# Reordering preparation work around the QK projection, the folds, the router and the last row sums of a gated attention and PEER kernel

## The chip, the cores and the metric

The kernel runs on one core of one Trainium2 chip. The metric is device time in microseconds (us) of one execution, lower is better. A profile is one execution recorded by the hardware profiler; its span is the time from the first to the last instruction.

## What is computed

One token sequence x (2048 tokens of 1024) goes through two branches, mixed by a gate for each token. Branch a is self-attention with 32 heads of 32; branch b is a PEER layer: each token, for each of 32 heads, picks one of 64 experts by two small argmaxes over 8 keys, and adds the expert's row of v, weighted by a GELU of its dot product with the expert's row of u.

```python
g = sigmoid((x * gate_w).sum(-1, keepdims=True))
# branch a
q, k, v = split_heads(x @ wqkv)
o = softmax(q @ k.T * 32 ** -0.5) @ v
a = merge_heads(o) @ wo
# branch b, K = 1
q = einsum("nd,dhc->nhc", x, w_q)                 # two halves of 128
i1 = argmax(q[..., :128] @ k1.T); i2 = argmax(q[..., 128:] @ k2.T)
e = i1 * 8 + i2                                   # the softmax over one candidate is 1
act = gelu(einsum("nd,nhd->nh", x, u[e]))
b = einsum("nh,nhd->nd", act, v[e])
out = g * a + (1 - g) * b
```

## The kernel before

All matrix products of the projections are made in fp32r from two parts of each operand: a high part (ScalarE copies the fp32 value into the narrower type) and a low part (VectorE subtracts the high part from the value). A product takes three matmuls for each slice of the contraction: high by high, high by low, low by high. The helpers are `hi_of` (L134) and `lo_of` (L137) for parts, `x_hi`, `x_lo`, `w_hi`, `w_lo`, `w_parts` for those of one operand, and `split` (L93) for both at once.

The order of the instructions on each engine is the order in which the program writes them: the schedule is written by hand. Within an engine each instruction waits for those before it, and DMAs stand in the queue of the engine that issues them (SyncE by default, ScalarE or GpSimd where named).

**QK projection** (0 to about 382 us). The 2048 columns of the Q and K weights are eight chunks; the tokens are two passes of 1024. A unit is one chunk (a Q and a K block) by one pass. Units 0 and 8, the first of each pass, are computed plainly (`plain_mm`, `plain_group`) and leave through `plain_evac`; all others, `unit(u)` (L472), are one step of Strassen's scheme in Winograd's form: seven products P1 to P7 of half-size operands, of which some are sums (S1 to S4 of the weights, T1 to T4 of x). `product` (L286) makes one, twelve matmuls of 512 columns into a PSUM bank; six banks are used in turn. The order in a unit is P1, P5, P6, P2, P7, P3, P4. VectorE adds the products up, and `evac` (L248) writes a result as two parts to DRAM: the high part, then what is left over in the list `late` from the evacuation before (`run_late`, L239: a sum of squares on ScalarE that also reads the bank or writes over it, L246, and two DMAs on ScalarE's queue), then the low part. A bank is free for another product only when its squares are done. Between the products stand the turns: `ready(name)` prepares operands of the next unit, and `hook(name)` runs steps put down in `hooks` for one unit and product. The raw tiles are used again: T1 takes the place of B11, T3 of B12, T2 of B22, T4 of B21 in pass 0.

**Folds.** The PEER query weights are folded with the keys into 448 columns, since only differences of key scores are needed. `fold()` (L320) makes two of 32 parts by matmuls with `kpad`; after each fourth part ScalarE copies the bank to `wt` (L336) and the step goes on a list; `load_wqs` then loads the raw weights for the next two. `FOLDS` names the units with a fold at the end, `MID_FOLDS` those with one more after P2. `fold_t()` (L341), behind P5 of the next unit, transposes the copied bank on TensorE (L348), copies it out (L351) and writes it to the DRAM tensor `WPD` on GpSimd's queue. The 64 columns of u complete WPD; they are copied from DRAM to DRAM at L400.

**Router** (382 to about 470 us). `open_rw` (L646) loads WPD and `hi_wp`, `lo_wp` split it. For each tile of 128 tokens `router_mm` (L702) makes 24 matmuls, then `router_step(t)` (L754) runs a pipeline over tiles: `router_1` (ScalarE copies the u scores, VectorE finds maxima and marks them, GpSimd multiplies by ranks), `router_2` (VectorE), `router_3` (GpSimd), `router_4` (VectorE). Between the steps stand splits of the x tiles of other token quarters (`split_rx`, loaded by `load_rx`), and `bound` (L759) makes from the maxima of the squares (`sq`, `amax`, `pr`, `prm`) a limit for the scores. At t = 8 the program branches on it: `exact_maxima` (L775), with the branch at L786.

**Values and attention.** The V projection follows, then 32 heads of attention from 638 us to about 1670: scores to a ring of PSUM banks (L1286), exponentials on ScalarE (L1296), products with V (L1307), row sums by VectorE and DMA adds.

**Output projection.** The last head's row sums (`norm_sums`, L1354) go to DRAM (`smd`) and come back (`load_r`, `rr<-smd`), are turned into factors (`norm_r`) and come back again spread over the partitions (`rb`, `accd`). Until they are there the projection works on the other heads (`wo_mm`, L1486), with the PEER part from `load_at` (L1482) through `av_mm`; then it takes the last group (`split_o`, L1558).

Of the kernel before, what the change touches and what calls it, by code (L numbers as in the profile page):

```python
# [19 lines left out]
KC = D // 128  # L20
# [11 lines left out]
def gated_mha_peer_kernel(ctx, tc, xT, wqkv, wv, wo, wq, k12, ug, v, out):  # L32
# [367 lines left out]
    dma(WPD[:, :, 448:], ug.rearrange("p (k m) -> p k m", k=KC)[:, :, :64], nc.gpsimd)  # L400
# [3 lines left out]
    for kc in range(KC):  # L404
        if kc:
            split_x(kc)
        if kc in (1, 2):
            split_w0(2 * kc, 2 * kc + 2 if kc == 1 else KC)
        if kc + 4 < KC:
            load_x(0, kc + 4)  # L410
        if kc == 3:
            load_w(1)
        if kc == 4:
            for n in range(2):
                load_wq(n)
        if kc == HC:
            gate_mm(range(HC))
        if kc == KC - 2:
            gate_mm(range(HC, KC))
        if kc == KC - 1:  # L420
            x_sum(0, "T1")
            w_hi(1, "A11")
            x_hi(0, "T1")
            x_sum(0, "T3")
            w_lo(1, "A11")
            x_lo(0, "T1")
            w_sum(1, "S1")
            w_hi(1, "S1")
            w_sum(1, "S3")
            x_sum(0, "T2")  # L430
            w_lo(1, "S1")
            x_hi(0, "T2")
            w_sum(1, "S2")
            w_hi(1, "S2")
            w_lo(1, "S2")
            x_lo(0, "T2")
        order = [(n, i) for i in range(3) for n in range(2)]
        if kc in (0, KC - 1):
            order = [(n, i) for n in range(2) for i in range(3)]
        for w in range(2):  # L440
            for n, i in order:
                plain_mm(w, n, kc, i, kc == 0 and i == 0, kc == KC - 1 and i == 2)
# [5 lines left out]
    hooks = {}  # L448
    w_hi(1, "A12")
    w_lo(1, "A12")  # L450
    plain_evac(0, 1, 0)
    gate_out(0)
    x_sum(0, "T4")
# [5 lines left out]
    w_lo(1, "S3")  # L459
    w_hi(1, "S4")  # L460
    x_hi(0, "T4")
    w_lo(1, "S4")
    hooks[1, "P1"] = [(x_lo, 0, "T4"), (plain_evac, 0, 1, 1)]
    hooks[1, "P5"] = [(w_parts, 1, "A22"), (plain_evac, 0, 0, 0)]
# [3 lines left out]
    MID_FOLDS = {4, 10, 13}  # L468
# [3 lines left out]
    def unit(u):  # L472
# [69 lines left out]
        evac(1, c, n0, u2, p4)  # L542
        hook("P4")
        ready("P4")
        if u in FOLDS:
            fold(u != KC - 2)
# [80 lines left out]
    hooks[9, "P1"] = [(plain_evac, KC, 1, 1), (w_parts, nxt, "A22")]  # L627
# [16 lines left out]
    Wp, rwp = [], []  # L644

    def open_rw():  # L646
        wr.close()
        wqp.close()
        rw = Pool("rw", side="right")
        wpl, wph = ([rw.tile([128, HC, 512], F32R, name=f"wp{part}{i}") for i in range(2)] for part in "lh")  # L650
        for i in range(2):
            dma(wpl[i], WPD[:, i * HC:(i + 1) * HC, :])
            Wp.extend((wph[i][:, k, :], wpl[i][:, k, :]) for k in range(HC))
        rwp.extend((rw, wph, wpl))

    def hi_wp(i):
        hi_of((rwp[1][i],), rwp[2][i].bitcast(F32))

    def lo_wp(i):
        lo_of((rwp[1][i], rwp[2][i]), rwp[2][i].bitcast(F32))  # L660
# [9 lines left out]
    rw = rwp[0]  # L670
    assert not hooks and fold_no[0] == 32 and not pending


    blk = const.tile([128, 4], F32, name="blk")
    nc.vector.tensor_reduce(blk, ident.rearrange("p (j r) -> p j r", j=4), axis=AX.X, op=OP.max)
    pr = const.tile([128, KC], F32, name="pr")
    amax = const.tile([128, 2, KC], F32, name="amax")
    nc.vector.tensor_reduce(amax, sq, axis=AX.X, op=OP.max)
    nc.vector.tensor_mul(pr, amax[:, 0, :], amax[:, 1, :])
    nc.scalar.activation(pr, pr, AF.Sqrt)  # L680
    prm = const.tile([128, KC, 4], F32, name="prm")
    nc.vector.tensor_mul(prm, pr[:, :, None].to_broadcast([128, KC, 4]),
                         blk[:, None, :].to_broadcast([128, KC, 4]))
# [183 lines left out]
    rw.close()  # L867

# [870 lines left out]
```

## Time and profile before

| | us |
|---|---|
| three runs | 1853.41, 1857.26, 1858.73 |
| median | 1857.26 |
| profiled execution, its own time | 1857.74 |
| its span | 1856.0 |
| TensorE busy | 1826.5 |
| VectorE busy | 1457.1 |
| ScalarE busy | 1312.7 |
| GpSimd busy | 173.6 |
| mean granted TensorE clock | 0.994 |

A row of a timeline gives the start in us from the span's beginning, the length in us, the engine, the line of the program, the operation, output and inputs, how many were merged, and in brackets the engine's idle time just before and what ended it. A row of the list of waits gives who waited for whom, the total in us, how many times, and the longest. A row of a stretch gives for each engine the busy time and the number of instructions, then the granted TensorE clock (1.00 is full), the busy share of the 16 DMA engines and GB/s. PE is TensorE, DVE VectorE, ACT ScalarE, POOL GpSimd, SP SyncE. A row of a DMA queue gives packets, MB, and the share of all 16 engines' time in the stretch asked for.

### The profile page before, as it was taken

The numbers are of one execution on the slowest core, as the hardware profiler recorded it, in microseconds if no ns is written. First come the engines' busy times: TensorE is split into PE (matmuls) and PEld (weight loads), VectorE is DVE, ScalarE is ACT, GpSimd is POOL, SyncE is SP. The second block draws the span as 40 slices with busy tenths as digits, with TensorE's granted clock in tenths as the row PEclk, the third lists the DMA queues.
The fourth block names the chain that finished last, engine by engine and source line by source line (L and its number), as shares of the span: only waits on it lengthen the run. The fifth ranks groups of instructions, "written<-read, shape, count | busy, mean of one in ns | idle before, by whom it ended". The sixth has DMA issues, their size and how long they took to land.

```text
span 1856.0 us, 26459 instructions
## 1 busy us (share of the span) xinstructions
PE 1826.5 (98%) x10083; PEld 1106.0 (60%) x10083; DVE 1457.1 (79%) x1258; ACT 1312.7 (71%) x1716; POOL 173.6 (9%) x230
## 2 busy tenths in 40 slices
PE   9899999998999999999999999999999999999999
PEld 6677767787888744444444444444444444446887
DVE  7765875678877788888888888888888888884575
ACT  5544554441233499999999999999999999992221
POOL 1000000035301200000000000000000000000000
PEclk9999999999999999999999999999999999999999
DMA  7687697753247677767677777777777777775872
GB/s 266 201 282 257 233 290 248 229 177 104 80 140 253 240 174 159 177 155 180 156 183 174 161 183 165 184 172 180 166 178 169 163 161 180 185 135 165 278 174 82
DMA packets 135633, 345.24 MB, mean 186 GB/s; under 512 B 17168, under 2 KB 57904, under 8 KB 116112
## 3 DMA queue, kind: packets, MB, share of 16 engines
q1 hardware_dynamic: 95696, 193.41, 35.1%
q0 software_dynamic: 17984, 112.36, 27.9%
q10 hardware_dynamic: 21824, 37.76, 6.8%
q8 instruction: 80, 1.31, 0.3%
q14 instruction: 49, 0.40, 0.1%
HBM read 171.76 MB, written 72.36 MB: 132 GB/s over the span
## 4 chain that ended last, share of the span: by engine, by line
PE 63%; issue 7%; DMA 2%; DVE 2%; POOL 1%; ACT 1%; SPq 0%; DVEq 0%; POOLq 0%; ACTq 0%
PE ring L1286 27%; PE o L1307 25%; PE pa L932 6%; PE pa L1491 1%; PE ring L1320 1%; PE bk L709 1%; PE pa L1498 1%; DVE acc L1336 1%; DMA smd<-ssb 1%; DMA rb<-rd 1%; POOL eq L723 1%; DMA accd<-rd 0%; DMA t1l<-xl 0%; DVE xl L95 0%; DVE xh L938 0%
## 5 line engine op out<-in xcount | busy, mean ns | idle before, releaser
L1296 ACT ACTIVATE P<-ring 128x1024 f32<-128x1024 f32 (+2 forms) x1031 | 913.0, 985 | 14.6 <-DMA accd<-P 1.1
L1336 DVE TENSOR_TENSOR acc<-acc,P 128x2048 f32<-128x2048 f32 x319 | 730.9, 2291 | 73.2 <-ACT P L1296 48.0
L1307 PE MATMUL o<-P,V 128*32 128x512 f32 x3840 | 464.8, 599 | 0.0
L1286 PE MATMUL ring<-Q,K 98*128 98x512 f32 x1024 | 272.5, 407 | 0.5 <-ACT P L1296 0.5
L1286 PE MATMUL ring<-z,z 98*128 98x512 f32 x1020 | 270.5, 407 | 0.6 <-ACT accd L1296 0.6
L1286 PEld LDWEIGHTS ring<-Q,K 98*128 98x128 f32 x1024 | 181.9, 188 | 145.3 <-ACT P L1296 73.3
L1286 PEld LDWEIGHTS ring<-z,z 98*128 98x128 f32 x1020 | 181.4, 188 | 142.5 <-ACT P L1296 72.3
L1307 PEld LDWEIGHTS o<-P,V 128*32 128x32 f32 x3840 | 98.8, 109 | 223.3 <-issue 214.4
L1329 POOL DMA_DIRECT2D accd<-P x95 | 81.5, 857 | 931.7 <-ACT P L1296 414.0
L1334 DVE TENSOR_TENSOR acc<-P,P 128x2048 f32<-128x2048 f32 x32 | 73.4, 2292 | 74.5 <-ACT P L1296 74.5
L292 PE MATMUL bk<-xh,S 128*128 128x512 f32 x336 | 83.7, 401 | 2.8 <-ACT bk L246 2.8
L292 PE MATMUL bk<-xh,A 128*128 128x512 f32 x336 | 82.8, 395 | 0.0
L292 PE MATMUL bk<-xl,S 128*128 128x512 f32 x336 | 80.2, 390 | 2.2 <-ACT bk L246 2.2
L292 PEld LDWEIGHTS bk<-xh,A 128*128 128x128 f32 x336 | 62.1, 188 | 23.8 <-issue 7.5
L135 ACT ACTIVATE hi<-u 128x512 fp32r<-128x512 f32 x42 | 26.5, 632 | 69.5 <-DVE u L498 68.0
L292 PEld LDWEIGHTS bk<-xh,S 128*128 128x128 f32 x336 | 64.0, 193 | 17.4 <-ACT bk L246 3.3
L292 PEld LDWEIGHTS bk<-xl,S 128*128 128x128 f32 x336 | 62.9, 188 | 17.3 <-ACT bk L246 2.6
L1339 DVE TENSOR_TENSOR acc<-acc,accd 128x2048 f32<-128x2048 f32 x32 | 73.1, 2284 | 0.0
L1296 ACT ACTIVATE accd<-ring 128x1024 f32<-128x1024 f32 (+2 forms) x64 | 62.3, 1034 | 2.3 <-PE ring L1286 2.2
L932 PE MATMUL pa<-woh,acc 128*128 128x512 f32 x192 | 62.2, 389 | 0.0
L138 DVE TENSOR_TENSOR A<-wraw,A 128x512 fp32r<-128x512 f32 x42 | 28.9, 688 | 32.0 <-ACT A L135 32.0
L498 DVE TENSOR_TENSOR u<-u,bk 128x512 f32<-128x512 f32 x70 | 46.6, 682 | 5.3 <-PE bk L292 2.6
(300 smaller groups left out, 2138.9 us busy)
## 6 DMA issues: line engine op xcount, KB each, us to landing
accd<-P POOLq DMA_DIRECT2D x95, 1024.0 KB, 7.6
wqt<-in_wq SPq DMA_DIRECT2D x64, 512.0 KB
wraw<-in_wqkv SPq DMA_DIRECT2D x28, 512.0 KB
kdh<-hi ACTq DMA_DIRECT2D x32, 256.0 KB
kdl<-lo ACTq DMA_DIRECT2D x32, 256.0 KB
qdh<-hi ACTq DMA_DIRECT2D x32, 256.0 KB
qdl<-lo ACTq DMA_DIRECT2D x32, 256.0 KB
z<-kdh SPq DMA_DIRECT2D x32, 256.0 KB
```

Of the source, the lines that this page charges most:

```text
L135: nc.scalar.activation(parts[0], src, AF.Copy)
L138: nc.vector.tensor_tensor(out=parts[1], in0=src, in1=parts[0].bitcast(F32), op=OP.subtract)
L292: nc.tensor.matmul(ps, a[i][:, k, :], b[j][:, k, :], start=(k == 0 and i == j == 0), stop=(k == HC - 1 and i == 1))
L498: nc.vector.tensor_tensor(out=out, in0=a, in1=b, op=OP.add)
L932: nc.tensor.matmul(ps, self.a[a][i][:, k, :], self.b[b][j][k], start=(not first and k == 0 and i == j == 0), stop=(k == HC - 1 and i == 1))
L1286: on_ring(nc.tensor.matmul(ring[:, i, :], K[:98, kt * 128:(kt + 1) * 128], Q[:98, qc * 512:(qc + 1) * 512], start=True, stop=True), i)
L1296: on_ring(nc.scalar.activation(P[h, kt][:, q0 * 512:(q0 + m) * 512].rearrange("p (a m) -> p a m", a=m), ring[:, i:i + m, :], AF.Exp, scale ...
L1307: nc.tensor.matmul(O[h][32 * qc:32 * qc + 32, :], Vt[g][:, kt, 32 * j:32 * j + 32], p[:, qc * 512:(qc + 1) * 512], start=(kt == 0), stop=( ...
L1329: nc.gpsimd.dma_start(ACCD[h], P[h, kt], accum_op=OP.add)
L1334: nc.vector.tensor_add(ACC[h], P[h, 0], P[h, kt])
L1336: nc.vector.tensor_add(ACC[h], ACC[h], P[h, kt])
L1339: nc.vector.tensor_add(ACC[h], ACC[h], ACCD[h])
```

## The change

It adds and removes no matmul. In the order of the program:

- The copy of u's columns into `WPD` moves from the beginning of GpSimd's queue to behind unit 0's evacuations.
- The operand steps between units 0 and 1 are written in another order. They were ahead of the last group of plain matmuls in the text and are now behind it, which by itself changes no engine's order; the sum T4 comes before S2, the first steps of A12 before those of S2, `x_lo` of T4 out of unit 1; a `run_late` comes before S4's low part, and one behind A22's parts in units 1 and 9; A22 moves from P5's hook to P1's in unit 1.
- A unit's fold comes before P4's hook and turn, no longer after them; the middle fold of unit 10 moves to unit 11.
- `WPD` is loaded behind P6 of unit 14 into a pool in the place of the folds' loads (`load_wp`, pool `rwl`); its split and that of the x tile `n1` (`hi_n1`, `lo_n1`) are spread over unit 15, where `n1` was split behind the unit.
- The norms' small steps move from in front of the router to its steps 2 and 3 (`norms`, `spread_norms`); `router_step` runs `router_1` of the new tile before `router_2` of the one before.
- `load_at` for the first two token blocks comes behind `load_r` of the last row sums.

```diff
-    dma(WPD[:, :, 448:], ug.rearrange("p (k m) -> p k m", k=KC)[:, :, :64], nc.gpsimd)
...
-        if kc == KC - 1:
-            x_sum(0, "T1")
...
-            w_sum(1, "S3")
-            x_sum(0, "T2")
-            w_lo(1, "S1")
-            x_hi(0, "T2")
-            w_sum(1, "S2")
-            w_hi(1, "S2")
-            w_lo(1, "S2")
-            x_lo(0, "T2")
...
     hooks = {}
+    x_sum(0, "T1")
...
+    w_sum(1, "S3")
+    x_sum(0, "T2")
+    w_lo(1, "S1")
+    x_hi(0, "T2")
+    x_sum(0, "T4")
+    w_sum(1, "S2")
     w_hi(1, "A12")
+    w_hi(1, "S2")
+    x_lo(0, "T2")
+    w_lo(1, "S2")
     w_lo(1, "A12")
     plain_evac(0, 1, 0)
     gate_out(0)
-    x_sum(0, "T4")
     x_hi(0, "T3")
     x_lo(0, "T3")
     plain_evac(0, 0, 1)
     w_hi(1, "S3")
     w_sum(1, "S4")
     w_lo(1, "S3")
+    x_hi(0, "T4")
     w_hi(1, "S4")
-    x_hi(0, "T4")
+    run_late()
     w_lo(1, "S4")
-    hooks[1, "P1"] = [(x_lo, 0, "T4"), (plain_evac, 0, 1, 1)]
-    hooks[1, "P5"] = [(w_parts, 1, "A22"), (plain_evac, 0, 0, 0)]
+    x_lo(0, "T4")
+    hooks[1, "P1"] = [(plain_evac, 0, 1, 1), (w_parts, 1, "A22"), (run_late,)]
+    hooks[1, "P5"] = [(plain_evac, 0, 0, 0)]
+    dma(WPD[:, :, 448:], ug.rearrange("p (k m) -> p k m", k=KC)[:, :, :64], nc.gpsimd)
...
-    MID_FOLDS = {4, 10, 13}
+    MID_FOLDS = {4, 11, 13}
...
         evac(1, c, n0, u2, p4)
+        if u in FOLDS:
+            fold(u != KC - 2)
         hook("P4")
         ready("P4")
-        if u in FOLDS:
-            fold(u != KC - 2)
...
-    hooks[9, "P1"] = [(plain_evac, KC, 1, 1), (w_parts, nxt, "A22")]
+    hooks[9, "P1"] = [(plain_evac, KC, 1, 1), (w_parts, nxt, "A22"), (run_late,)]
...
-    def split_n1():
-        XS.update({(0, 0): X["B11"], (0, 1): X["B21"], (1, 1): X["B22"],
-                   (1, 0): x_parts("xh1", XR["n1"], xp)})
+    def hi_n1():
+        XS.update({(0, 0): X["B11"], (0, 1): X["B21"], (1, 1): X["B22"], (1, 0): x_parts("xh1", None, xp)})
+        hi_of(XS[1, 0], XR["n1"])
+
+    def lo_n1():
+        lo_of(XS[1, 0], XR["n1"])
+
+    def load_wp():
+        wqp.close()
+        pools.append(Pool("rwl", side="right"))
+        for i in range(2):
+            wl_.append(pools[0].tile([128, HC, 512], F32R, name=f"wpl{i}"))
+            dma(wl_[i], WPD[:, i * HC:(i + 1) * HC, :])
 
     def open_rw():
         wr.close()
-        wqp.close()
-        rw = Pool("rw", side="right")
-        wpl, wph = ([rw.tile([128, HC, 512], F32R, name=f"wp{part}{i}") for i in range(2)] for part in "lh")
-        for i in range(2):
-            dma(wpl[i], WPD[:, i * HC:(i + 1) * HC, :])
...
+        pools.append(Pool("rw", side="right"))
+        wh_.extend(pools[1].tile([128, HC, 512], F32R, name=f"wph{i}") for i in range(2))
...
-    hooks[14, "P1"] = [(load_n1,)]
-    hooks[15, "P1"] = [(open_rw,)]
-    hooks[15, "P2"] = [(hi_wp, 0), (lo_wp, 0)]
-    hooks[15, "P7"] = [(hi_wp, 1), (lo_wp, 1)]
+    hooks[14, "P6"] = [(load_n1,), (load_wp,)]
+    hooks[15, "P1"] = [(open_rw,), (hi_wp, 0)]
+    hooks[15, "P5"] = [(lo_wp, 0), (hi_wp, 1)]
+    hooks[15, "P6"] = [(lo_wp, 1), (hi_n1,)]
+    hooks[15, "P2"] = [(lo_n1,)]
...
     run_late()
-    split_n1()
...
     def router_step(t):
-        for lag, f in ((3, router_4), (2, router_3), (1, router_2), (0, router_1)):
+        for lag, f in ((3, router_4), (2, router_3), (0, router_1), (1, router_2)):
...
+    def norms():
+        nc.vector.tensor_reduce(blk, ident.rearrange("p (j r) -> p j r", j=4), axis=AX.X, op=OP.max)
+        nc.vector.tensor_reduce(amax, sq, axis=AX.X, op=OP.max)
+        nc.vector.tensor_mul(pr, amax[:, 0, :], amax[:, 1, :])
+        nc.scalar.activation(pr, pr, AF.Sqrt)
+
+    def spread_norms():
+        nc.vector.tensor_mul(prm, pr[:, :, None].to_broadcast([128, KC, 4]),
+                             blk[:, None, :].to_broadcast([128, KC, 4]))
...
         router_step(t)
+        if t == 2:
+            norms()
+        if t == 3:
+            spread_norms()
         if t == 4:
             bound()
...
     load_o(1, 0, KC - 1, nc.gpsimd)
-    for n in range(2):
-        load_at(n)
     split_hi(1)
     for kc in range(1, KC - 1):
         split_hi(kc + 1)
         if kc == 1:
             norm_sums(H - 1, sm)
             load_r(G - 1)
+            for n in range(2):
+                load_at(n)
             pso.close()
```

More of the change, by code (lines that the diff above doesn't have):

```diff
@@ L448, in gated_mha_peer_kernel @@
     hooks = {}
+    x_sum(0, "T1")
+    w_hi(1, "A11")
+    x_hi(0, "T1")
+    x_sum(0, "T3")
+    w_lo(1, "A11")
+    x_lo(0, "T1")
+    w_sum(1, "S1")
+    w_hi(1, "S1")
+    w_sum(1, "S3")
[4 more added lines that the diff above has]
+    w_sum(1, "S2")
     w_hi(1, "A12")
+    w_hi(1, "S2")
+    x_lo(0, "T2")
+    w_lo(1, "S2")
     w_lo(1, "A12")
@@ L638, in load_n1 @@
         XR["n1"] = load_quarter(1, 0, x8.tile([128, HC, 512], F32, name="x8"))
[L640 to L644 removed]
+    def hi_n1():
[3 more added lines that the diff above has]
+        lo_of(XS[1, 0], XR["n1"])
+    wl_, wh_, pools = [], [], []
+    def load_wp():
[4 more added lines that the diff above has]
+            dma(wl_[i], WPD[:, i * HC:(i + 1) * HC, :])
     def open_rw():
         wr.close()
[L648 to L654 removed]
+        pools.append(Pool("rw", side="right"))
+        wh_.extend(pools[1].tile([128, HC, 512], F32R, name=f"wph{i}") for i in range(2))
     def hi_wp(i):
[L657 removed]
+        hi_of((wh_[i],), wl_[i].bitcast(F32))
     def lo_wp(i):
[L660 to L665 removed]
+        lo_of((wh_[i], wl_[i]), wl_[i].bitcast(F32))
+    hooks[14, "P6"] = [(load_n1,), (load_wp,)]
[3 more added lines that the diff above has]
+    hooks[15, "P2"] = [(lo_n1,)]
     for u in range(KC + 1, NUNIT):
@@ L668, in gated_mha_peer_kernel @@
     run_late()
-    split_n1()
-    rw = rwp[0]
+    rwl, rw = pools
+    Wp = [(wh_[i][:, k, :], wl_[i][:, k, :]) for i in range(2) for k in range(HC)]
     assert not hooks and fold_no[0] == 32 and not pending
     blk = const.tile([128, 4], F32, name="blk")
-    nc.vector.tensor_reduce(blk, ident.rearrange("p (j r) -> p j r", j=4), axis=AX.X, op=OP.max)
     pr = const.tile([128, KC], F32, name="pr")
     amax = const.tile([128, 2, KC], F32, name="amax")
-    nc.vector.tensor_reduce(amax, sq, axis=AX.X, op=OP.max)
-    nc.vector.tensor_mul(pr, amax[:, 0, :], amax[:, 1, :])
-    nc.scalar.activation(pr, pr, AF.Sqrt)
     prm = const.tile([128, KC, 4], F32, name="prm")
-    nc.vector.tensor_mul(prm, pr[:, :, None].to_broadcast([128, KC, 4]),
-                         blk[:, None, :].to_broadcast([128, KC, 4]))
     prf = prm.rearrange("p c j -> p (c j)")
@@ L867, in gated_mha_peer_kernel @@
     rw.close()
+    rwl.close()
     zp = Pool("zp", side="right")
```

7 lines of the change are left out of this document (removed).

## The prediction

> **What bounds the kernel now.** I read the page's first part, then the list of who waited for whom on TensorE, then the timelines of TensorE, ScalarE, VectorE and SyncE around each wait, and the DMA queues.
>
> ```profile
> PE 1826.5 (98%) x10083; PEld 1106.0 (60%) x10083; DVE 1457.1 (79%) x1258; ACT 1312.7 (71%) x1716; POOL 173.6 (9%) x230
> ```
> ```profile
> PE bk L348 <- ACT x L336: 5.4, 3, 3.9
> PE bk L292 <- ACT bk L246: 5.0, 2, 2.8
> PE bk L709 <- DVEq L786: 4.8, 1, 4.8
> PE pa L1491 <- ACT z L94: 4.4, 1, 4.4
> PE bk L280 <- ACT xh L94: 1.5, 1, 1.5
> ...
> PE bk L331 <- DMA wqt<-in_wq: 0.6, 1, 0.6
> PE bk L709 <- DVE wpl L138: 0.5, 1, 0.5
> ```
>
> TensorE is busy for all but 29.5 us of the 1856.0 us span, so nearly everything else is hidden behind it, and a change that adds no matmul can gain only in these waits (columns: us in total, times, longest). The seven rows hold 22.2 us. The change touches the place of each of them: line 348 is the transpose in `fold_t`, which waits for ScalarE's copy of the fold (L336); line 292 is a QK product that waits until a bank's squares (L246) are done; L709 with L786 is the router at the branch of `exact_maxima`; L1491 is the output projection; L280 the very first products.
>
> A long wait costs more than itself:
>
> ```profile
> 52.52 3.01 PE L292 MATMUL bk<-xh,S 128*128 128x512 f32 x12 [2.83 <-ACT bk L246]
> ...
> 72.43 1.11 PE L348 MATMUL bk<-ident,x 128*128 128x128 f32 x4 [3.90 <-ACT x L336]
> 73.20 5.22 PE L292 MATMUL bk<-xh,S 128*128 128x512 f32 x12
> ```
> ```profile
> 70.00:80.00 10.00, 7.57 (x24) 6.20 (x25) 7.20 (x12) 6.21 (x14) 0.80 (x1) 0.66 0.96 301
> ```
>
> After 2.83 us of idle time twelve matmuls take 3.01 us; after 3.90 us the next twelve take 5.22, and the granted clock of that stretch is 0.66. So a wait of 3.90 carries a surcharge of 2.2 us, one of 2.83 none. I take 3.4 us, the middle, as the point from which the surcharge falls due.
>
> **A, the folded weights' load out of the first microseconds.**
>
> ```profile
> wpd<-in_ug POOLq DMA_DIRECT2D x1, 256.0 KB, 5.5
> ```
> ```profile
> q0 software_dynamic: 61, 0.12, 40.2%
> ```
> ```profile
> q0 software_dynamic: 83, 0.15, 25.6%
> ```
> ```profile
> 8.20 0.63 ACT L94 ACTIVATE xh<-xh 128x512 fp32r<-128x512 f32 x1 [2.34 <-DMA xh<-in_xT]
> ```
>
> The two queue rows are the stretches 4 to 6 and 6 to 8 us: GpSimd's queue, nearly all of it this one 256 KB copy, takes 0.80 + 0.51 = 1.3 us of all 16 engines just while ScalarE waits for the second half of the first x tile, and TensorE behind it for 1.5 us. Bounds of the gain: 0 (if the x load was not behind it) and 1.5; I take **1.1**, near the queue's own 1.3. In its new place the copy stands on GpSimd's queue behind the four gate writes, beside unit 1's products; what it delays there by 1.3 us (the next fold's weights) is used a whole unit of seven products later. Without that cover it costs 1.3.
>
> **B, the turns ahead of unit 1, and the fold ahead of P4's turn.**
>
> ```profile
> 43.48 1.92 ACT L135 ACTIVATE xh<-xh 128x2048 fp32r<-128x2048 f32 x1 [3.96 <-DVE x L152]
> ```
> ```profile
> 40.51 0.68 DVE L138 TENSOR_TENSOR lo<-bk,hi 128x512 fp32r<-128x512 f32 x1
> 41.11 2.28 DVE L152 TENSOR_TENSOR x<-x,xh 128x2048 f32<-128x2048 f32 x1
> ```
> ```profile
> 71.29 0.61 ACT L135 ACTIVATE S<-wraw 128x512 fp32r<-128x512 f32 x1
> 71.81 0.57 ACT L336 ACTIVATE x<-bk 128x512 f32<-128x512 f32 x1
> ```
>
> Before, T3's high part (43.48) waits 3.96 us for the sum T4 (41.11), which stands on VectorE behind T2's low part, three short weight steps, a wait for one of them and an evacuation (40.51). The change puts that sum in front of them. Counting VectorE's instructions again in the new order (a wide one holds it 2.2 to 2.3 us, a narrow one 0.60, from 40.51 to 41.11), the sum is done before 37.5 and T2's low part, whose raw tile T3's high part overwrites, at 40.2. So T3's high part starts at about 40.3, 3.2 us earlier, and everything in order behind it with it. The new `run_late` behind A22 takes back 0.5: its write of a low part stands in ScalarE's queue until VectorE has made that part, and the next evacuation's copy is queued behind. Left: 2.7. Two waits follow from this. The squares that held P7 (2.83 us) now run before P7 comes: that wait goes whole. Then `fold_t` in unit 2 is late next: its copy at 71.81 stood behind two weight copies at 0.52 each (71.29 is the second); it now stands ahead of them, so it ends 2.7 + 1.04 = 3.7 earlier, while TensorE arrives 2.8 earlier. The wait of 3.90 becomes 3.0, TensorE goes on 3.7 earlier, and if 3.0 stays below the 3.4 also without the slow dozen: 3.7 + 2.2 = **5.9**. Bounds 3.2 (no more than the chain's shift) and 6.9.
>
> **C, units 9 to 13.** The second wait on squares (5.0 - 2.8 = 2.2) stands in unit 9; the added `run_late` lets those squares run before the next evacuation, so it goes. But again `fold_t` comes next:
>
> ```profile
> 255.22 0.57 ACT L336 ACTIVATE x<-bk 128x512 f32<-128x512 f32 x1
> ```
>
> Its copy moves ahead of two weight copies here too, 1.04 us, and no more, since VectorE's chain there doesn't move: of the 2.2 only **1.0** is kept. The third such wait (unit 13, the longer of the 1.5 that the two others share, 1.1) has one copy less in front: **0.5**. The fold moved from unit 10 to unit 11 leaves unit 10's wait for weights (0.6), yet unit 11 gets the same close pair of folds: between 0 and 0.6, I take **0.3**.
>
> **D, unit 15 and the router.**
>
> ```profile
> 394.68 16.11 SPq L76 DMA_DIRECT2D rx<-in_xT  x4
> ```
> ```profile
> 399.61 1.92 ACT L94 ACTIVATE xh<-rx 128x2048 fp32r<-128x2048 f32 x1 [3.96 <-DMA rx<-in_xT]
> ```
> ```profile
> 427.35 0.22 ACT L713 ACTIVATE xu<-bk 128x64 f32<-128x64 f32 x1 [5.22 <-PE bk L709]
> 432.79 0.22 ACT L713 ACTIVATE xu<-bk 128x64 f32<-128x64 f32 x1 [5.22 <-PE bk L709]
> ```
> ```profile
> 392.36 2.29 DVE L95 TENSOR_TENSOR xh<-x,xh 128x2048 fp32r<-128x2048 f32 x1 [2.49 <-ACT xh L94]
> ...
> 413.14 0.61 DVE L717 TENSOR_REDUCE m<-bk 128x64 f32<-128x448 f32 x1
> ...
> 419.69 0.61 DVE L717 TENSOR_REDUCE m<-bk 128x64 f32<-128x448 f32 x1
> ...
> 437.03 0.22 DVE L722 TENSOR_SCALAR eq<-m 128x64 f32<-128x64 f32 x1
> ```
>
> TensorE makes a router tile each 5.44 us (427.35 to 432.79). VectorE is finished with tile 7 at 437.25, 8 us after it could be, and the branch holds TensorE from 432.8 until then. The lag is there from the start: tile 0 is ready 8 x 5.44 us before 432.79, at 389.3, while VectorE is busy with n1's split until 394.65 and then with the norms. The change does that split inside unit 15, where VectorE has no weights to prepare, and starts the weight split a product earlier; VectorE is then free at about 386, before tile 0. SyncE's rx loads, which start at 394.68, the moment that split frees its raw tile, go out some 9 us earlier and land before 395, when step 1 asks for them. From there: a step that holds a split takes 6.55 us (413.14 to 419.69), 4.26 without its 2.29, of which I count 0.5 as waiting for GpSimd that the new order takes out. Seven steps to tile 7 are 7 x 3.8 + 4 x 2.2 (splits) + 0.9 (norms) + 1.0 (bound) = 37.3 us, in 38.1 available; the square root, now in front of a split on ScalarE, adds about 2. So VectorE passes the branch at 430.5 to 431.5 and TensorE arrives at 432.3. I leave 0.3 us for the branch (437.25 to 437.52 now). Gain: 4.8 - 0.3, the 0.5 of the wpl wait, and the surcharge 2.2 of a wait longer than 3.9: **7.2**. Bounds 0.5 and 7.5.
>
> **E, the last row sums.**
>
> ```profile
> 1674.10 3.74 SPq L76 DMA_DIRECT2D at<-atd  x2
> 1677.93 1.15 SPq L76 DMA_DIRECT2D smd<-ssb  x1
> 1689.13 0.31 SPq L76 DMA_DIRECT2D rr<-smd  x1
> ```
> ```profile
> DMA packets 27, 0.05 MB, mean 25 GB/s; under 512 B 1, under 2 KB 4, under 8 KB 27
> ```
> ```profile
> DMA packets 17, 0.02 MB, mean 8 GB/s; under 512 B 3, under 2 KB 16, under 8 KB 17
> ```
>
> The two loads stand on SyncE's queue in front of the write of the last sums (smd), on which the 4.4 us wait hangs. They hold it up by some 2.4 us at issue. But the write lands only at 1689.1, and the packet rows of 1686 to 1688 and 1688 to 1690 show why: a trickle of 2 KB packets (an earlier write) until 1688, then 1 KB packets (the two loads) for about 0.7 us, then the sums. Issued earlier, they still stand behind the 2 KB packets. Gain **0.7** (bounds 0.5 and 2.4); the wait becomes 3.7, above 3.4, and keeps its surcharge. The loads, now behind the wait for smd, come late by at most what the same wait covers.
>
> **The sum** is 1.1 + 5.9 + 1.8 + 7.2 + 0.7 = 16.7 us. The profiled execution took 1857.74 us (span 1856.0), 0.5 above the median of the three runs, 1857.26; nothing in the attention stage is touched, so it moves as a whole: 1857.74 - 16.7 = 1841.0, or 1840.5 by the median.
>
> **The rivals.** *The clock falls after the 3.0 us wait too.* For it: 3.0 is near 3.4. Then 2.2 less: 1842.7. Chance 0.18.
>
> *The clock looks at fixed stretches of time.* If what counts is an idle stretch of fixed length on a grid that doesn't know the kernel, then a wait of 3.7 us mostly straddles two, and E's surcharge goes as well: 1838.3. Against it: 3.90, 4.4 and 4.8 are only a little longer, and 3.90 was enough. Chance 0.13. The Trainium skill, "TensorE: Matmul & The Clock Gate", Part 1, says that: a free-running window of about 3.4 us, and half rate after an idle one; its sum would be the 1838.3, and the trace agrees with it at 2.83 and speaks half against it at 3.90, which would seldom hold a whole window.
>
> *VectorE still comes late to the branch*, because the rx loads are held by another tile of the closed pools and land near 399.6 as now. Then the square root's stall is added to the old lag and D gives no more than the 0.5: 1840.5 + 6.7 = 1847.2. Chance 0.12.
>
> *Slower: VectorE becomes the router's bound.* The new order makes each step wait for its tile first; if GpSimd's product beside VectorE's two-input instructions stretches every step to the 6.55 us of one with a split, the 15 tiles behind the first take 15 x 1.11 = 16.7 us more, and D's 7.2 is lost: 1840.5 + 23.9 = 1864.4. It decides from a mean step over 5.44. Against it: my count is 37.3 in 38.1. Chance 0.05.
>
> *The change moves waits and no more*: other in-order work turns up in each place, and the time stays within 3 us of before. Chance 0.05.
>
> **How the numbers follow.** My forecast has 0.47 and gives 1840.5 us. 0.3% is 5.6 us, about what a measurement of this kernel can tell from no change. Faster by more than that: 0.47 + 0.18 + 0.13 + 0.12 = 0.90; within: 0.05; slower: 0.05. The range takes in the three nearest rivals with the bounds of A and E: 1836.5 to 1849.5.
>
> **What would show it.** In the list of waits: L246 gone; L348 at about 3.0 + 1.5 + 0.6; DVEq L786 under 1 us; L1491 about 3.7; L280 under 0.6. The dozen after `fold_t` in unit 2 near 3.0 us, the router's first reduction near 388 before all shifts. Wrong: a wait on L786 of over 2 us, a copy L336 later than 69 us, a new wait on S3 or A22 in the units behind a fold, or an attention stage that isn't as long as before.

## The result and the profile after

The changed kernel takes 1848.07 us (median of 12 runs, 1844.77 to 1852.13) where the kernel before took 1857.08 beside it: a ratio of 0.9956, 95% interval 0.9946 to 0.9965. It is 9.0 us faster by the medians and 8.2 by the ratio (6.5 to 10.0). 16.7 were forecast. The profiled execution has a span of 1847.2 us against 1856.0.

The list of who waited for whom on TensorE, after (total us, times, longest):

```profile
PE bk L348 <- ACT x L336: 7.9, 3, 4.0
PE pa L1506 <- ACT z L94: 3.4, 1, 3.4
PE bk L771 <- DVE prm L766: 2.8, 1, 2.8
...
PE bk L280 <- ACT xh L94: 1.2, 2, 0.7
PE pa L947 <- ACT z L94: 1.2, 1, 1.2
...
PE bk L292 <- ACT bk L246: 0.3, 1, 0.3
```

The waits on squares (L246) and at the branch (L786 before) are gone but for 0.3 us each, as forecast. But the waits on the fold's copy (L348) grew from 5.4 to 7.9, and two rows are new: L771, the bound's matmuls, and a second wait on z at L947. The first products (L280) still wait 1.2 where under 0.6 was forecast.

TensorE's timeline, after, at P7 of unit 1, at the fold's transposes in units 2, 10 and 13, in the router, at the branch and in the output projection:

```profile
49.07 2.88 PE L292 MATMUL bk<-xh,S 128*128 128x512 f32 x12
...
69.00 1.11 PE L348 MATMUL bk<-ident,x 128*128 128x128 f32 x4 [4.03 <-ACT x L336]
69.76 5.39 PE L292 MATMUL bk<-xh,S 128*128 128x512 f32 x12
...
253.01 0.66 PE L348 MATMUL bk<-ident,x 128*128 128x128 f32 x4 [2.39 <-ACT x L336]
...
321.31 0.66 PE L348 MATMUL bk<-ident,x 128*128 128x128 f32 x4 [1.51 <-ACT x L336]
...
408.83 0.22 PE L771 MATMUL bk<-ones,prm 128*32 128x1 f32 x2 [2.85 <-DVE prm L766]
...
409.78 1.05 PE L709 MATMUL bk<-wph,xh 128*128 128x512 f32 x2
...
433.00 0.47 PE L709 MATMUL bk<-wph,xh 128*128 128x512 f32 x1 [0.30 <-ACT xu L713]
...
1688.12 1.19 PE L1506 MATMUL pa<-woh,z 128*128 128x512 f32 x4 [3.35 <-ACT z L94]
...
1725.71 3.29 PE L947 MATMUL pa<-wo_raw,z 128*128 128x512 f32 x12 [1.21 <-ACT z L94]
```

P7 of unit 1 no longer waits (49.07). The transposes wait 4.03 where 3.0 was forecast, and the dozen behind them is still slow (5.39). The two other waits of the transposes are 2.39 and 1.51 where 1.5 and 0.6 were forecast. In the router TensorE stands 2.85 us in front of the bound, and two matmuls behind it take 1.05 instead of 0.61 to 0.63: half rate. The branch costs 0.30.

To see where the time went I cut every profile at the same five places of TensorE's timeline and list the lengths between them: start to the first gate product (L190, part A), from there to the transposes of unit 7 (B), to the router's first matmul (C), to its last (D), and the rest, with E (us; the names are those of the runs below):

| kernel | A | B | C | D | rest |
|---|---|---|---|---|---|
| before | 21.42 | 163.03 | 197.86 | 95.84 | 1377.82 |
| before, copy moved | 20.75 | 160.46 | 199.21 | 95.41 | 1376.90 |
| before, loads moved | 21.37 | 160.36 | 199.89 | 96.09 | 1377.94 |
| before, router part alone | 21.36 | 163.29 | 199.00 | 87.89 | 1379.58 |
| changed | 21.16 | 160.33 | 196.98 | 92.50 | 1376.23 |
| changed, again | 20.07 | 159.64 | 197.52 | 92.34 | 1377.40 |
| bound later | 19.68 | 158.93 | 198.20 | 93.41 | 1376.20 |
| norms first | 19.00 | 158.49 | 196.65 | 87.99 | 1377.83 |
| norms first, C undone | 20.71 | 160.26 | 198.43 | 88.04 | 1377.87 |

Kernels that share the code of a part differ in it by 1 to 3 us from one execution to the next, D apart. So a part is sized by means over the kernels that share it, not by the two profiles alone.

### The profile page after: what moved, and what is told of

Its sections match the earlier page's. It is cut to its first block, busy times and chain, and to the rows that moved or that the text cites. A ratio compares the mean times of both kernels' runs of the same rounds, so it can differ in the third digit from the quotient of the medians.

```text
span 1847.2 us, 26455 instructions
## 1 busy us (share of the span) xinstructions
PE 1823.2 (99%) x10083; PEld 1103.8 (60%) x10083; DVE 1460.9 (79%) x1258; ACT 1313.8 (71%) x1716; POOL 162.1 (9%) x230
## 4 chain that ended last, share of the span: by engine, by line
PE 72%; DMA 5%; DVE 1%; ACT 1%; SPq 0%; issue 0%; DVEq 0%; ACTq 0%; POOLq 0%
PE ring L1301 27%; PE o L1322 25%; PE bk L947 6%; PE pa L947 6%; PE bk L709 3%; PE bk L966 2%; PE ring L1335 1%; DMA accd<-P 1%; DMA accd<-rd 1%; DMA smd<-ssb 1%; PE pa L1513 1%; DMA out<-rb 1%; DMA rx<-in_xT 1%; DMA rb<-rd 0%; SPq L76 0%; DMA V<-od 0%
## 5 line engine op out<-in xcount | busy, mean ns | idle before, releaser
L1344 POOL DMA_DIRECT2D accd<-P x95 | 81.5, 858 | 931.6 <-ACT P L1311 430.5
L947 PE MATMUL pa<-woh,acc 128*128 128x512 f32 x192 | 62.2, 389 | 0.0
L499 DVE TENSOR_TENSOR u<-u,bk 128x512 f32<-128x512 f32 x70 | 46.6, 682 | 3.6 <-PE bk L292 2.5
```

The lines of the kernel that those rows point to most:

```text
L499: nc.vector.tensor_tensor(out=out, in0=a, in1=b, op=OP.add)
L947: nc.tensor.matmul(ps, self.a[a][i][:, k, :], self.b[b][j][k], start=(not first and k == 0 and i == j == 0), stop=(k == HC - 1 and i == 1))
L1344: nc.gpsimd.dma_start(ACCD[h], P[h, kt], accum_op=OP.add)
```

## The experiments

### The router

**Norms first.** The norms go back ahead of the router; all else is the changed kernel.

```diff
+    norms()
+    spread_norms()
     for t in range(NT - 1):
...
-        if t == 2:
-            norms()
-        if t == 3:
-            spread_norms()
```

> The changed kernel with the norms, their square root and their spread made once ahead of the router's first step, as the kernel before had them. Theory (the wait for the norms at the bound is what took the router's gain): TensorE's 2.85 us wait on prm and the half-rate stretch behind it (1.6 us) go, VectorE fits the norms into its idle time ahead of tile 0 (2.01 us there, 0.9 needed), the branch is still reached in time; 1848.1 - 4.4 = 1843.7 us. Rival (VectorE is the router's bound with any order, since a step with a split takes 6.3 us against TensorE's 5.44): the wait comes back at the branch, L786, at 2 to 4 us, and the time stays within 1846.5 to 1848.5.

1845.84 us, 2 above what I had expected; ratio to before 0.9936 (0.9923 to 0.9950). Its list of waits begins:

```profile
PE bk L348 <- ACT x L336: 7.6, 3, 3.9
PE pa L945 <- ACT z L94: 4.0, 1, 4.0
PE pa L1504 <- ACT z L94: 1.5, 1, 1.5
```

No row for the bound, and the wait at the branch stays at 0.3. The router's matmuls in the view by line (duration ns minimum, median, longest; first and last start in us), changed kernel, then norms first:

```profile
L709 PE MATMUL bk<-wph,xh x128: 389/389/628, 378.5 to 468.3; 128*128 128x512 f32 x128
L709 PE MATMUL bk<-wph,xl x128: 388/389/389, 381.3 to 471.0; 128*128 128x512 f32 x128
```
```profile
L709 PE MATMUL bk<-wph,xh x128: 389/389/500, 374.1 to 459.4; 128*128 128x512 f32 x128
L709 PE MATMUL bk<-wph,xl x128: 388/389/389, 377.0 to 462.1; 128*128 128x512 f32 x128
```

From first to last: 92.5 us changed, 88.0 with the norms first. The 4.5 us are the 2.85 of the wait and the half-rate stretch behind it, as the theory had it. By the ratios against before the gain is 0.0020, 3.7 us; the two ratios' intervals reach 1.8 and 2.5 us to each side, so it is the trace more than the time that shows it.

**Bound later.** The norms stay in steps 2 and 3; the bound that reads them moves one tile on.

```diff
+        if t == 5:
+            bound()
         if t == 4:
-            bound()
             load_wv(0, "xh0")
```

> The changed kernel with the norms where the change put them and their consumer one step later: the bound's matmuls stand behind tile 5 instead of tile 4. Theory (two costs in one: TensorE's wait on prm, and VectorE's own lag from the norms and the square root): the 2.85 us wait on prm goes, but TensorE then reaches the branch some 4.4 us earlier while VectorE finishes tile 7 where it does now, so 2 to 3 us of wait turn up on L786, with a half-rate stretch if that fills most of a unit; the stretch from the router's first to its last matmul shrinks from 92.4 to 90 to 91.5 us, where the norms ahead of the router give 88.0. Rival (only the place of the consumer counts): 88.0, no wait on L786, time as with the norms first, about 1844.

1847.94 us, ratio 0.9947 (0.9934 to 0.9961). TensorE's timeline at the branch:

```profile
426.15 0.39 PE L709 MATMUL bk<-wph,xl 128*128 128x512 f32 x1
429.35 0.77 PE L709 MATMUL bk<-wph,xh 128*128 128x512 f32 x1 [2.81 <-DVEq L796]
...
430.33 1.06 PE L709 MATMUL bk<-wph,xh 128*128 128x512 f32 x2
```

The wait of 2.85 left the bound and came back as 2.81 at the branch, with half rate behind it; the router takes 93.4 us, 0.9 more than before this edit, where I had expected 90 to 91.5. So the place of the consumer is not the cause alone: VectorE is late at the branch too. Here it ends step 7 at 429.14, while TensorE was through at 426.54. VectorE's timeline in the changed kernel shows by what:

```profile
384.51 0.62 DVE L717 TENSOR_REDUCE m<-bk 128x64 f32<-128x448 f32 x1 [2.01 <-ACT xu L713]
...
389.95 0.62 DVE L717 TENSOR_REDUCE m<-bk 128x64 f32<-128x448 f32 x1 [3.79 <-ACT xu L713]
...
396.29 0.62 DVE L717 TENSOR_REDUCE m<-bk 128x64 f32<-128x448 f32 x1
...
399.71 0.28 DVE L760 TENSOR_REDUCE blk<-ident 128x4 f32<-128x128 f32 x1
...
402.39 2.29 DVE L95 TENSOR_TENSOR xl<-rx,xl 128x2048 fp32r<-128x2048 f32 x1 [2.08 <-ACT xl L94]
...
405.20 0.61 DVE L717 TENSOR_REDUCE m<-bk 128x64 f32<-128x448 f32 x1
...
408.59 0.18 DVE L766 TENSOR_TENSOR prm<-pr,blk 128x32 f32<-128x32 f32 x1
...
431.14 0.28 DVE L738 SCALAR_TENSOR_TENSOR p<-mm 128x32 f32<-128x32 f32 x2
```
```profile
400.34 0.21 ACT L763 ACTIVATE pr<-pr 128x8 f32<-128x8 f32 x1 [3.68 <-DVE pr L762]
400.46 1.90 ACT L94 ACTIVATE xl<-rx 128x2048 fp32r<-128x2048 f32 x1
```

(VectorE, then ScalarE; each L717 row is the beginning of a router step.) The square root stands in ScalarE's queue ahead of the split's high part, and itself waits for VectorE's short steps; VectorE then idles 2.08 us for that high part. The step takes 8.9 us (396.29 to 405.20) where a step with a split takes 6.3, and the last of the norms, prm, comes at 408.59, while TensorE was through with tile 4 at 406.0.

**Router part alone**, on the kernel before, with the norms first: does D hold without the changed front? Its edit is that of the router and unit 15 in the change, with `norms()` and `spread_norms()` ahead of the loop as above.

> The kernel before with part D alone, its norms kept ahead of the router's first step. Theory (the forecast's D was right in all but the place of the norms): the wait on L786 falls from 4.8 to 0.3, the wpl wait of 0.5 goes, the half-rate stretch goes, no wait on prm: 7.2 us, up to 8.5, less than before: 1857.1 - 7.2 = 1849.9 to 1848.6. Rival (VectorE has the time only because the changed front feeds it earlier): a wait of 1 to 3 us stays at the branch, 1852 to 1854.

1850.63 us, ratio 0.9961 (0.9947 to 0.9975): 6.8 less by the medians (1857.45 beside it). No wait at the bound, 0.3 at the branch; the router's stretch is 87.9 us, 7.9 under the mean of the three kernels that have the old one (95.8). The theory holds: with the norms ahead of the loop, D is worth the 7.2 to 8.5 that was expected, also without the changed front.

### The fold's copy in unit 2

**Without the run_late behind A22.** In this part all kernels but one have the norms first.

```diff
-    hooks[1, "P1"] = [(plain_evac, 0, 1, 1), (w_parts, 1, "A22"), (run_late,)]
+    hooks[1, "P1"] = [(plain_evac, 0, 1, 1), (w_parts, 1, "A22")]
```

> The changed kernel with the norms ahead of the router and without the added run_late behind A22 in unit 1. Forecast on record: that call takes back 0.5 us; the changed kernel's trace shows ScalarE held 1.47 us by it and VectorE 1.0. Theory (1.0): VectorE's chain comes 1.0 us earlier, the fold's copy with it, the wait in unit 2 falls from 3.9-4.0 to about 3.0, unless the squares, now late, hold the seventh product again (a wait on L246 of up to 1.5). Rival (0.5): the wait falls to 3.5. Time within 1.5 us of the norms alone, 1844.

1844.38 us, ratio 0.9932 (0.9919 to 0.9946). TensorE's timeline, and two stretches of 3.4 us around it:

```profile
66.74 0.76 PE L348 MATMUL bk<-ident,x 128*128 128x128 f32 x4 [3.00 <-ACT x L336]
67.16 4.58 PE L292 MATMUL bk<-xh,S 128*128 128x512 f32 x12
```
```profile
63.70:67.10 3.40, 0.40 (x4) 0.36 (x4) 1.84 (x3) 2.22 (x5) 0.00 (x0) 1.00 1.04 415
67.10:70.50 3.40, 3.40 (x11) 2.72 (x10) 2.42 (x4) 3.19 (x8) 0.00 (x0) 0.51 0.99 287
```

The wait falls by 1.0 to 3.00, and no wait on squares returns: the call cost 1.0 us, not the 0.5 of the forecast. And 3.00 us of wait still bring one stretch at half rate (0.51), so the forecast's threshold of 3.4 us for the length of a wait is refuted too. (The third number from the end is the granted clock.) The kernel before shows the other side, in stretches cut on the grid of 3.413 us on which its recorded clock changes. Of the 2.83 us ahead of P7, 1.0 and 1.8 fall into two stretches, and the clock stays; of the 3.90 us ahead of the transposes, 2.7 fall into one, and the next runs at half rate:

```profile
47.30:50.70 3.40, 2.39 (x11) 1.64 (x9) 2.92 (x5) 1.75 (x2) 0.00 (x0) 1.00 0.11 44
50.70:54.10 3.40, 1.58 (x7) 1.32 (x8) 2.68 (x2) 3.26 (x7) 0.00 (x0) 1.00 0.40 114
54.10:57.50 3.40, 3.40 (x17) 2.82 (x16) 3.29 (x6) 0.72 (x3) 0.00 (x0) 1.00 0.75 151
67.80:71.20 3.40, 0.74 (x4) 0.27 (x2) 2.48 (x4) 1.98 (x5) 0.00 (x0) 0.99 1.02 414
71.20:74.60 3.40, 2.17 (x7) 1.91 (x8) 1.87 (x3) 3.40 (x9) 0.00 (x0) 0.50 1.06 292
```

**Copy first in unit 1.** The fold's copy goes ahead of the last evacuation in ScalarE's queue.

```diff
         p4 = product("P4")
+        if u == 1:
+            fold()
         add(u2, u2, p4)
         evac(1, c, n0, u2, p4)
-        if u in FOLDS:
+        if u in FOLDS and u != 1:
             fold(u != KC - 2)
```

> The changed kernel with the norms ahead of the router and, alone of the fold's edits, the fold's copy of unit 1 issued on ScalarE ahead of the last evacuation instead of behind it. Theory (the copy stands in ScalarE's queue behind an evacuation that waits for VectorE's sum): the copy runs at 45.9 to 46.5 us after the gate instead of 47.2, TensorE's wait in unit 2 falls from 3.9-4.0 to 1.4-2.5, no or one half-rate unit: the stretch from the gate to the transposes of unit 5 falls from 116.8 to 113-114.5 us and stays so; 1844 - 3 = 1841. Rival (what is gained there is given back ahead of the second x pass): 1844.

1843.76 us, ratio 0.9931 (0.9918 to 0.9945). The wait in unit 2 falls to 1.30, as the theory says, and the transposes run 45.1 us after the gate product instead of 47.7. But the gain does not stay: the next fold's copy is then late, in unit 4.

```profile
109.43 0.96 PE L348 MATMUL bk<-ident,x 128*128 128x128 f32 x4 [2.06 <-ACT x L336]
```

The wait there is 2.06 us, with a stretch at half rate behind it, and length B is 159.1 us, no less than with the norms alone (158.5). My theory fell; the rival was right, only the place was nearer.

**Transposes behind P6**, in all units, on the changed kernel as it is (the norms not moved).

```diff
         p5 = product("P5")
-        fold_t()
...
         p6 = product("P6")
+        fold_t()
```

> The changed kernel with the transposes of the fold queued on TensorE behind the sixth product instead of behind the fifth (2.72 us later in its order). Theory (the copy that fold_t waits for is the checkpoint that absorbs the gains ahead of it): the wait in unit 2 falls from 4.0 to about 1.3, those of units 10 and 13 (2.4 and 1.5) go, the half-rate stretch behind the first goes (2.3): 1848.1 - 2.7 - 2.3 - 2.4 - 1.5 = 1839.2 at best, and at least 5 us less, 1843. Rival (VectorE's chain behind the copy is as late): waits of 2 to 4 us on a bank's squares or a sum turn up within the same unit, and the time falls by 2 at most, to 1846.

1849.99 us, ratio 0.9957 (0.9943 to 0.9971): no gain. The waits on the copy shrink from 7.9 to 1.1, and others stand in their place:

```profile
PE bk L771 <- DVE prm L766: 2.8, 1, 2.8
PE bk L709 <- ACT bk L246: 2.7, 1, 2.7
PE bk L280 <- DVE S L138: 2.6, 1, 2.6
```

L280 is the first product group of unit 8 (at 198.28), which waits for the low part of the weights in S4's tile; L709 the router's first bank (at 377.69). This was the rival's case, though the waits came units later and not within the same one.

**Transposes behind P6 in units 2, 10 and 13 only, with the copy first and the norms first.**

> The changed kernel with the norms ahead of the router, with the fold's copy of unit 1 on ScalarE ahead of the last evacuation, and with the transposes behind the sixth product in units 2, 10 and 13 only, so that all three waits on the fold's copy (7.9 us in sum) go. Theory (they are checkpoints, and the second x pass and the router's start are the next ones): the gain shrinks to 0 to 2 us by the router's first tile, time 1842 to 1844 where the norms alone give about 1844. Rival (they are true costs): 7.9 and the half-rate stretch of 2 less, 1834.

1841.63 us, ratio 0.9915 (0.9902 to 0.9928). Length B is 154.8 us, C 197.0: the front gives 4 to 5 us beyond the kernel with the norms first (4.7 by the mean of B, 4.2 by the medians). I had expected 0 to 2; it is not 8 either.

**The same with unit 4 added** (units 2, 4, 10 and 13; the transposes' part of the edit, against the changed kernel):

```diff
-        fold_t()
+        if u not in (2, 4, 10, 13):
+            fold_t()
...
         p6 = product("P6")
+        if u in (2, 4, 10, 13):
+            fold_t()
```

> The kernel with the norms first, the copy first and the later transposes in units 2, 10 and 13 (1841.6 measured), with those of unit 4 later as well. Its wait on the copy in unit 4 (1.4 us) goes: 1840.2. Rival (given back ahead of the second x pass): 1841.6.

1839.47 us, ratio 0.9908 (0.9892 to 0.9925), the fastest: some 17 us under before. Unit 2, where TensorE waited 3.90 and 4.03 us:

```profile
64.12 2.88 PE L292 MATMUL bk<-xh,S 128*128 128x512 f32 x12
66.84 0.60 PE L348 MATMUL bk<-ident,x 128*128 128x128 f32 x4
67.20 3.02 PE L292 MATMUL bk<-xl,A 128*128 128x512 f32 x12
```

Its step from the kernel with three units, 2.2 us, lies within the intervals; length B is no shorter (155.3), so that the last edit gains anything is not shown.

### Parts A, C and E

**Copy moved alone** (A), on the kernel before.

```diff
-    dma(WPD[:, :, 448:], ug.rearrange("p (k m) -> p k m", k=KC)[:, :, :64], nc.gpsimd)
     dma(kraw, k12.rearrange("p (a e) -> p a e", a=2), nc.gpsimd)
...
+    dma(WPD[:, :, 448:], ug.rearrange("p (k m) -> p k m", k=KC)[:, :, :64], nc.gpsimd)
     load_w(2)
     fold()
```

> The kernel before with part A alone: the folded weights' copy moved behind the first turns. Theory (absorbed): the second half of the first x tile comes 0.9 us earlier as in the changed kernel, but VectorE's chain of sums does not move, so the seventh product of unit 1 still starts at 52.4 to 52.6 and its wait on the squares is longer by what was gained; time 1857.1, no change. Forecast on record: 1.1 us less, the product at 51.4, 1856.0.

1856.29 us, ratio 0.9994 (0.9984 to 1.0004): the time alone does not tell the gain from none. TensorE's timeline:

```profile
51.83 5.49 PE L292 MATMUL bk<-xh,S 128*128 128x512 f32 x12 [2.83 <-ACT bk L246]
```

P7 of unit 1 starts 0.69 earlier than before, and the gate product 0.67 earlier: what the start gains is handed on, since VectorE's sums hang on the same x tiles (the first of them runs at 22.9 instead of 23.6). The theory that it would be absorbed fell. Over all profiles the gate product starts at 21.36 to 21.42 us with the copy in its old place (three) and at 19.00 to 21.16 with it moved (eleven), 20.2 in the mean: A is worth some 1.2 us at that point.

**C undone**, with the norms first.

```diff
-    MID_FOLDS = {4, 11, 13}
+    MID_FOLDS = {4, 10, 13}
...
-        if u in FOLDS:
+        if u in FOLDS and u < 8:
             fold(u != KC - 2)
         hook("P4")
         ready("P4")
+        if u in FOLDS and u > 8:
+            fold(u != KC - 2)
...
-    hooks[9, "P1"] = [(plain_evac, KC, 1, 1), (w_parts, nxt, "A22"), (run_late,)]
+    hooks[9, "P1"] = [(plain_evac, KC, 1, 1), (w_parts, nxt, "A22")]
```

> The changed kernel with the norms ahead of the router and part C undone (no added run_late in unit 9, the fold behind P4's turn from unit 9 on, the middle fold in unit 10). Theory (C's gain on the squares is given back at the next fold's copy): the wait on the squares returns at about 2.2, the fold's wait in unit 10 falls from 2.4 to about 0.5, and the stretch from unit 3 to the router's first tile is as long as with C, within 0.7 us: same time as the norms alone, 1844. Forecast on record: C is worth 1.8, so 1845.8.

1847.26 us, ratio 0.9948 (0.9935 to 0.9961), 1.4 above the norms alone by the medians. The wait on squares comes back at 3.28 with a slow dozen behind it, and the wait on the copy in unit 10 is gone:

```profile
239.78 4.49 PE L292 MATMUL bk<-xl,S 128*128 128x512 f32 x12 [3.28 <-ACT bk L246]
...
254.56 0.60 PE L348 MATMUL bk<-ident,x 128*128 128x128 f32 x4
```

Length C is 198.4 without the edits. With them and the norms first it is 196.65 here, 1.8 us less, but 196.65 to 198.20 over the six kernels that keep units 9 to 15 as changed and have no transposes moved, 197.3 in the mean: 1.1 less. The theory that it is all given back is not borne out; the size is no better known than to a microsecond.

**Loads moved alone** (E): `load_at` goes behind `load_r`, as in the change, on the kernel before.

> The kernel before with part E alone: the two loads at behind the row sums' reciprocal. Theory (gained, then partly given back): the 4.4 us wait of the output projection falls to 3.3 to 3.4, and about 1.2 us come back at a later wait on z, some 36 us on, because the loads of od land no earlier; the time falls by 0 to 1, to 1856 to 1857, and by 0.8 more if the half-rate stretch behind the wait is one unit of 3.4 us and not two. Forecast on record: the wait becomes 3.7, no later wait, two slow units as before, 1856.4.

1856.67 us, ratio 0.9994 (0.9985 to 1.0003). TensorE's timeline:

```profile
1694.54 1.19 PE L1491 MATMUL pa<-woh,z 128*128 128x512 f32 x4 [1.48 <-ACT z L94]
...
1732.74 3.65 PE L932 MATMUL pa<-wo_raw,z 128*128 128x512 f32 x8 [3.27 <-ACT z L94]
```

The first wait fell by 3.0, not 1.1, and the second is 3.27, so the sum is 4.75 against 4.43 before. Over all profiles the two waits add up to 4.4 to 5.8 us without E (three: 4.43 before, 2.90 and 1.64 with the copy moved, 3.99 and 1.79 with the router part alone) and to 3.6 to 5.6 with it (eleven: changed 3.35 and 1.21, norms first 1.45 and 3.96), 4.9 and 4.6 in the mean. In this run the first gain is taken back by the second wait; a gain of E is not shown.

**The changed kernel again.**

> The changed kernel itself once more, beside the next three on the same chip. If the first loads differ from one execution to the next, TensorE's first gate product starts anywhere from 19.0 to 21.4 us, and the end moves with it; the stretch from the fold's transposes in unit 2 to the router's last tile copy and from there to the end should repeat within 1 us. Time 1848 (1846 to 1850).

1849.07 us, ratio 0.9957 (0.9944 to 0.9969). The start moved by 1.1 us (A 20.07); B, C and D repeat within 0.7 each, the rest within 1.2, a little more than the 1 us that I had allowed.

## Why the prediction was wrong

The sum by parts, as means over the kernels that share a part:

| part | forecast | measured | from |
|---|---|---|---|
| A | 1.1 | 1.2 | 21.4 - 20.2 |
| B | 5.9 | 2.3 | 161.8 (four) - 159.5 (five) |
| C | 1.8 | 1.7 | 199.0 (four) - 197.3 (four) |
| D | 7.2 | 3.4 | 95.8 (three) - 92.4 (two) |
| E | 0.7 | not shown (0.9, in spreads of 2.7 and 1.7) | 1378.1 (three) - 1377.2 (six) |
| sum | 16.7 | 9.5 | time: 9.0 (by the ratio 8.2) |

Two terms were mis-sized, B and D, and they make up nearly all of the miss.

**D: a deadline was overlooked, and VectorE's count was short.** The step that failed is the norms: they were counted as 0.9 us of VectorE and a stall of 2 us, and who reads them was not asked. TensorE does, behind tile 4, four tiles ahead of the branch. With prm at 408.59 it waited 2.85 us and took the half rate with it. "Norms first" gives those 4.5 us back, and "bound later" shows that to move only the reader moves only the wait.

The count up to the branch failed too, though the wait there is only 0.3. The forecast put VectorE through the branch 41.2 to 42.2 us after tile 0 (389.3 to 430.5 and 431.5), ahead of TensorE at 43.0. After, it takes 47.2 (tile 0's u scores are copied at 384.26, VectorE's step 7 ends at 431.4); that 431.4 lies within the forecast's own figures is chance, since tile 0 came 5.0 us earlier than in the kernel before. TensorE waits little there only because the bound had held it. With the bound later VectorE takes 46.6 (382.58 to 429.14), TensorE 44.0, and the wait is 2.81; with the norms first VectorE takes 43.0 (380.11 to 423.16). The seven steps up to tile 7 were counted as 39.3 us (37.3 and 2) and took 43.05 (384.51 to 427.56): the step with the norms and the stall came as counted (8.9), but the first took 5.44 and not 3.8, since VectorE has nothing to do for 3.79 us until TensorE has made tile 1, and each of the others 0.3 to 0.6 more than counted.

**B: the wait at the copy did not shrink.** The forecast had TensorE 2.8 us earlier at the transposes and the copy 3.7, so 3.90 would become 3.0. Counted from the gate product, so without A's share, TensorE came 3.30 earlier (47.11 to 43.81): with the wait of 2.83 went some 0.5 us of gaps between the products around it. The copy came 3.18 earlier (50.39 to 47.21). The turns themselves came as worked out, with T3's high part at 40.52 us of the span where 40.3 was forecast; but the new `run_late` held VectorE for 1.0 and not 0.5:

```profile
50.86 0.58 ACT L246 ACTIVATE bk<-bk 128x512 f32<-128x512 f32 x1 [1.47 <-DVE lo L138]
...
68.37 0.57 ACT L336 ACTIVATE x<-bk 128x512 f32<-128x512 f32 x1
```

(ScalarE's timeline, after.) So the wait became 4.03 and the surcharge stayed, some 2.2 us in the forecast. That was the largest part of B's miss, and nothing in the forecast's list of rivals said that both sides would move together. The surcharge also had been read off one execution: in all three other kernels with the old front half rate followed P7's wait of 2.83 us as well, and the wait at the copy paid for it (1.00, 2.28 and 2.27 in place of 3.90). Two of these four have a length B of 160.4, so the old front's loss depends on where half rate falls, and B's 2.3 is a mean over that.

**The clock.** The rival "the clock looks at fixed stretches" was right in kind, and a threshold on the length of a wait was wrong: 3.00 and 2.06 us brought half rate, and the same 2.83 us ahead of P7 brought it in three executions and not in the fourth, the one that the forecast read. The Trainium skill ("TensorE: Matmul & The Clock Gate", Part 1) gives a free-running window of about 3.4 us and half rate after an idle one. The traces agree on the window; a whole idle one is not needed (below). What the rival said of E is not shown: the changed kernel has one slow stretch there instead of two, but so has the copy moved alone, without E, and "norms first, C undone", with E, has two.

**What held, and what held by luck.** A, in the mean. C's order of events too: the squares' wait goes, and the copy in unit 10 comes next. C's sum agrees by luck, since its terms do not. The waits at the copies of units 10 and 13 were to be 1.5 and 0.6 us and are 2.39 and 1.51, so they take back about 0.9 each that the forecast had kept. On the other side the squares' wait in unit 9, 2.19 in the execution that the forecast read, is 3.28 to 3.98 in the four other kernels without C's edits, each time with a slow stretch behind it that the forecast did not count. E's first wait is shorter (3.35, forecast 3.7), and the second at L947, which the forecast did not see, takes 1.21. In unit 15 and the router the earlier split did free the raw tile: the rx loads go out at 382.4 instead of 394.7 us, and the first reduction runs at 384.5 (forecast near 388 before all shifts; the router begins 3.8 earlier). So neither the rival of late rx loads nor that of a router with VectorE as its bound came, though the first one's 1847.2 lies nearest to the measured time.

Left open: what sets the second wait on z. In the changed kernel's trace the split that it waits for stands on ScalarE behind two copies that had waited 3.48 and 0.55 us for writes of the output (`out<-rb`), and with the norms first it waits for VectorE in the end. No run moved these.

## What to carry to other kernels

When a step is moved to a later place, list its readers on every engine and when each arrives; the nearest one sets the deadline, not the wait you are curing. A wait shrinks only by the difference of two arrivals, so compute both, with everything that reaches each; if one edit brings both forward, its gain passes through and the wait stays. And size small parts over several executions: the same code differed by up to 2.9 us in one part here (B, 160.4 to 163.3).

## What the runs showed of the hardware

- In the recorded clock of all 14 profiles the half-rate stretches inside the span last 3.413 or 6.827 us and lie on a grid of 3.413 us that is not tied to the kernel. Of the grid's stretches at full rate, all 36 in which TensorE was idle for 59% or more were followed by one at half rate, none under 47%, and 4 of 13 in between. A second slow one followed wherever the first was itself idle for 20% or more (11 of 11; at 18 and 19% one of two). From the transposes of unit 2 to those of unit 4, where nothing waits ahead of the latter (twelve profiles), that is 42.8 to 42.9 us without a slow stretch, 44.1 to 44.6 with one, 45.2 to 45.6 with two. So a wait of 2 us can cost 1.2 to 1.7 us more, or nothing, by where it falls on the grid; each wait of 3.8 us or more was followed by half rate.
- The first loads differ between executions: with the copy moved, the first gate product started anywhere from 19.0 to 21.2 us (eleven profiles), and in two executions of the changed kernel at 21.16 and 20.07.
